# A gated decode block whose instructions a small recorder issues in place of the tile framework

## Chip, cores and metric

The kernel runs on one core of one Trainium2 chip. The metric is the time of one execution in device microseconds (us); before the change it is 376.34 us, the median of three runs (375.96 to 376.35). A profile of one further execution gives the instructions, the DMA transfers and the waits of that core. The engines are TensorE (PE; its weight loads are PEld), VectorE (DVE), ScalarE (ACT), GpSimd (POOL) and SyncE (SP). A q behind a name (SPq) means the engine's sequencer, which issues DMAs and handles semaphores.

## What is computed

One decode step for two sequences (B = 2, one token each, width D = 448): a layer norm, grouped-query attention over a cache of 4096 positions with 8 key heads and 16 query heads of width 256, and a bilinear gated feed-forward branch that multiplies the result of the attention.

```
xn = layernorm(x)                                     # 2 x 448
q  = xn @ wq                                          # 16 heads of 256, two per key head
p  = softmax(q . k_cache / 16)                        # over 4096 positions
s  = (p . v_cache) @ wo                               # 4096 -> 448
g  = silu(((xn @ w_gate) * (xn @ w_up)) @ w_down)     # 448 -> 1792 -> 448
out = x + s * g
```

All is float32. The two caches are 2 x 8 x 4096 x 256 numbers each, and every byte of them and of the weights is read once: the profile counts 158.56 MB read from memory.

## The kernel before

The work goes in 16 steps, one for each pair of a key head and a sequence (`N = 16`; `LAST = 14`). A step needs one key block and one value block, each 128 partitions by 8192 numbers (4 MB). `scores(i)` (L265) multiplies the query with the key block, 16 calls that appear as 32 matmul records, into a pair of PSUM banks, and DVE takes the maximum (L275). `softmax` (L285) spreads the maximum with two small matmuls (L287, L292), ACT takes the exponential (L295), and DVE transposes it (L298). `values(i)` (L309) multiplies that with the value block (L313). The loop (L366) runs `values(i)`, `scores(i + 1)`, the next loads, and `softmax(i + 1)`. The feed-forward branch and the second half of the queries run inside the loop at i = 0, 2 and 4, and the first half of the output projection at i = 8.

**Loads.** All loads but x are issued by SP in the order of the list `todo`. Two ring buffers hold 8 MB each: `v{i} k{i+1}` side by side, from the array vk. One slot holds the weights one after the other (wq0, then wgu, wdq, wo). The last two loads are cut: last0 (k15, v14) into two pieces, last1 (v15 and the rest of wo) into seven. `issue(n)` (L66) puts the next n of them on SP's queue; each waits there until the buffer that it overwrites has been read. There are 29 loads on SP (wq0, wqx, first, 14 of vk, wgu, wdq, wo, 2 of last0, 7 of last1), and two on ACT for the two rows of x (L106).

**Who orders the work.** Each engine runs its instructions in the order in which the program names them (`tc.manual_schedule()`). The tile framework allocates the buffers (L43 to L47), works out the dependencies, and sets the semaphores and waits. An instruction carries one wait; where it needs more, an EVENT_SEMAPHORE instruction in front of it carries them. The framework uses one counting semaphore for each compute engine and eight for DMAs in turn. A buffer that is allocated again waits for all readers of the whole old buffer.

**The two ends.** The program object (L471) starts with four constant fills on POOL and one meeting of all five engines: they drain and signal POOL, which releases them. Leaving the framework's context (L476) adds an end. SP waits for every semaphore of the framework, the store's among them; then the five engines meet, POOL clears the range of semaphores with one instruction, and the five meet again.

**The tail**, which the prediction follows: L313 for the last step, L410 (ACT scales the result), L322 (`combine`), L351 (`project`), L412 (DVE transpose), L356 (`project_last`), L239 (`spread`), L422 and L423 (gate and residual on DVE), and L424, the store of 57 KB on SP's queue.

```
    last ring load:   plan(f"v{LAST + 1} wo2", last1, [0, 4096, 7168, *(ROW + i * D for i in (0, 3, 6, 7, 8))])
    the end:          nc.vector.tensor_mul(gate, acc[:, :SL], gate)
                      nc.vector.tensor_add(gate, gate, xg)
                      nc.sync.dma_start(out, gate)
```

Of the kernel before, what the change touches and what calls it, by code (L numbers as in the profile page):

```python
# [1 line left out]

# [8 lines left out]
OP = mybir.AluOpType  # L11
# [24 lines left out]


# [3 lines left out]
@with_exitstack  # L41
def gated_decode_block(ctx: ExitStack, tc: tile.TileContext, x, first, vk, last0, last1, wq0, wqx, wdq, wo, wgu, out):
    nc = tc.nc  # L43
    ring = ctx.enter_context(tc.tile_pool(name="ring", bufs=2))
    slot = ctx.enter_context(tc.tile_pool(name="slot", bufs=1))
    const = ctx.enter_context(tc.tile_pool(name="const", bufs=1))
    work = ctx.enter_context(tc.tile_pool(name="work", bufs=2))  # L47
    psum = ctx.enter_context(tc.tile_pool(name="psum", bufs=1, space=bass.MemoryType.PSUM))
    ctx.enter_context(tc.manual_schedule())

    def two():
        return psum.tile([128, 2, 512], F32, name="s", bufs=2)


    def bank(name=None):
        return psum.tile([128, 512], F32, name=name, bufs=1) if name else two()[:, 0]


# [6 lines left out]
    def issue(n=1):  # L65
        for names, src, cuts in todo[:n]:  # L66
            weight = names[0].startswith("w")
            if weight:
                t = slot.tile([128, PART], F32, name="slot", align_bytes=512)
            else:  # L70
                t = ring.tile([128, 2 * ROW], F32, name="ring", align_bytes=512)
            width = ROW if not weight else src.shape[1] // len(names)
            for i, name in enumerate(names):
                loaded[name] = t[:, i * width:(i + 1) * width]
            if names == ["wd", "wq1"]:
                loaded["wd"], loaded["wq1"] = t[:, :14 * D], t[:, 14 * D:]
            for lo, hi in zip(cuts, cuts[1:]):
                nc.sync.dma_start(t[:, lo:hi], src[:, lo:hi])
            if names == ["wq0"]:
                at = src.shape[1]  # L80
                loaded["wqx"] = t[:, at:at + EXTRA * 512]
                nc.sync.dma_start(loaded["wqx"][:SIDE], wqx[:, :4])
        del todo[:n]
# [16 lines left out]
    def early():  # L100
        return [work.tile([128, 2, 512], F32, name=n, bufs=1)[:B] for n in ("p", "pT")]
# [3 lines left out]
    for b in range(B):  # L105
        nc.scalar.dma_start(x2[b:b + 1], x[b:b + 1])  # L106
    ident = const.tile([128, 128], F32)
    make_identity(nc, ident)
    one = const.tile([1, 1], F32)
    nc.vector.memset(one, 1.0)  # L110


    st = const.tile([B, 4], F32)
    xc = e0[:, 1, :D]
    sq = e1[:, 0, :D]
    eh = const.tile([B, 1], F32)
    nc.vector.memset(eh, -0.5)
    nc.vector.tensor_reduce(st[:, 0:1], x2, axis=AX.X, op=OP.add)
    nc.vector.tensor_scalar(st[:, 1:2], st[:, 0:1], 1.0 / D, None, op0=OP.mult)
    nc.vector.tensor_scalar(xc, x2, st[:, 1:2], None, op0=OP.subtract)  # L120
    nc.vector.scalar_tensor_tensor(sq, xc, 1.0, xc, op0=OP.mult, op1=OP.mult, accum_out=st[:, 2:3])  # L121
    nc.vector.tensor_scalar(st[:, 3:4], st[:, 2:3], 1.0 / D, EPS, op0=OP.mult, op1=OP.add)
    rstd = const.tile([B, 1], F32)
    nc.gpsimd.tensor_tensor(rstd, st[:, 3:4], eh, op=OP.pow)
# [3 lines left out]
    nc.vector.tensor_scalar(xn[:, :D], xc, rstd, None, op0=OP.mult)  # L128
    nc.vector.tensor_scalar(xn[:, D:D + LEFT], xc[:, D - LEFT:], rstd, None, op0=OP.mult)
    nc.vector.tensor_scalar(xn[:, D + LEFT:], xc[:, 384:D - LEFT], rstd, None, op0=OP.mult)  # L130
    pt = bank()
    for k in range(NK):
        nc.tensor.transpose(pt[:, B * k:B * (k + 1)], xn[:, k * 128:(k + 1) * 128], ident[:B, :B])  # L133
    def copies(dst, pt):
        n, b = pt.shape
        nc.vector.tensor_copy(dst.rearrange("p k (b j) -> p k b j", b=B),
                              pt.rearrange("p (k b) -> p k b", b=B)[:, :, :, None].to_broadcast([n, b // B, B, DUP]))

    xnT = const.tile([128, NK - 1, W], F32)
    copies(xnT, pt[:, :(NK - 1) * B])  # L140

    oT1 = const.tile([128, 3, 2, REP, W], F32)
# [3 lines left out]
    nc.vector.memset(xf, 0.0)  # L146
# [6 lines left out]
    for j in range(NS):  # L153
        at = 384 + j * SIDE
        nc.tensor.transpose(pt[:SIDE, B * j:B * (j + 1)], xn[:, at:at + SIDE], ident[:B, :B])
    nc.tensor.transpose(pt[:2 * LEFT, B * NS:B * (NS + 1)], xn[:, D - LEFT:D + LEFT], ident[:B, :B])
# [5 lines left out]
    nc.gpsimd.affine_select(out=xl, in_=xl, compare_op=OP.is_ge, fill=0.0, base=0, pattern=[[-LEFT, 2], [0, W]],  # L162
                            channel_multiplier=1)
    nc.gpsimd.affine_select(out=xl, in_=xl, compare_op=OP.is_ge, fill=0.0, base=LEFT - 1, pattern=[[LEFT, 2], [0, W]],
                            channel_multiplier=-1)

    both = work.tile([128, D], F32, name="h")[:B, :W].rearrange("p (b j) -> p b j", b=B)
    nc.vector.tensor_copy(both, ident[:B, :B, None].to_broadcast([B, B, DUP]))
    pt = bank()
    for c in range(NT):  # L170
        nc.tensor.matmul(pt[W * c:W * (c + 1), :SL], both.rearrange("p b j -> p (b j)"), x2[:, c * SL:(c + 1) * SL],
                         start=True, stop=True)
    xg = const.tile([128, SL], F32)
    nc.vector.tensor_copy(xg, pt[:, :SL])

    pick = const.tile([128, B], F32)
    nc.vector.tensor_reduce(pick, ident.rearrange("p (c b j) -> p b j c", c=NT, b=B)[:, :, 0, :], axis=AX.X, op=OP.add)
    rows4 = const.tile([128, 2, REP], F32)  # L180
    nc.vector.tensor_reduce(rows4.rearrange("p e r -> p (e r)"),
                            ident.rearrange("p (c f j) -> p f j c", c=NT, f=4)[:, :, 0, :], axis=AX.X, op=OP.add)
    add_head = const.tile([128, NT, REP, DUP], F32)
    nc.vector.tensor_copy(add_head, pick[:, None, :, None].to_broadcast([128, NT, REP, DUP]))

    add_step = const.tile([128, 2 * NT, REP, 8], F32)
    nc.vector.tensor_copy(add_step, pick[:, None, :, None].to_broadcast([128, 2 * NT, REP, 8]))
    add_blocks = const.tile([128, 2, REP, DUP], F32)
    nc.vector.tensor_copy(add_blocks, rows4[:, :, :, None].to_broadcast([128, 2, REP, DUP]))

    def rows(ps, w, n, extra=None):
# [5 lines left out]
        for k in range(3):  # L197
            for c in range(NT):
                nc.tensor.matmul(ps[W * c:W * (c + 1), :n], xnT[:, k, :], block(NT * k + c), start=k == 0, stop=False)  # L199
        def last(a, i):  # L200
            nc.tensor.matmul(ps[64 * a:64 * (a + 1), :n], xf.rearrange("p a j -> p (a j)"), block(i), start=False, stop=True)  # L201

        if extra is not None:

            for j in range(NS):
                for c in range(2):
                    at = (c * NS + j) * n
                    nc.tensor.matmul(ps[W * c:W * (c + 1), :n], xeT[:, j, :], extra[:SIDE, at:at + n], start=False, stop=False)  # L208
                if j == 0:
                    last(1, 12)  # L210
            nc.tensor.matmul(ps[:2 * W, :n], xl.rearrange("p a j -> p (a j)"), extra[:2 * LEFT, 2 * NS * n:(2 * NS + 1) * n],  # L211
# [6 lines left out]
    qT = [const.tile([128, B, 4, 2, REP, DUP], F32, name=f"qT{h}") for h in range(2)]  # L218

    def query(h):  # L220
        ps = bank()
        rows(ps, loaded[f"wq{h}"], 512, None if h else loaded["wqx"])
        for r in range(REP):
            nc.vector.transpose(qT[h][:, :, :, :, r, :].rearrange("p b g d j -> p (g d) b j"),
# [3 lines left out]
    gate = const.tile([128, SL], F32)  # L228
    hT = const.tile([128, 14, W], F32)


    def lift(ps):
        t = work.tile([128, D], F32, name="h")
        nc.vector.tensor_copy(t, ps[:, :D])
        return t

    def spread(t, dst, start, stop):
        for n in range(NT):
            nc.tensor.matmul(dst[W * n:W * (n + 1), :SL], add_head[:, 0].rearrange("p r j -> p (r j)"),  # L239
                             t[:, n * SL:(n + 1) * SL], start=start, stop=stop)  # L240

    def ffn_in():
# [3 lines left out]
        g = work.tile([128, FC], F32, name="h")  # L246
        nc.scalar.copy(g, pp[:, 0, :FC])
        h = work.tile([128, FC], F32, name="h")
        nc.vector.tensor_mul(h, pp[:, 1, :FC], g)
        nc.vector.transpose(hT.rearrange("p i m -> p (i m)"), h)  # L250

    def ffn_out():
        ps = bank()
        for i in range(14):
            t = i % NT
            nc.tensor.matmul(ps[W * t:W * (t + 1), :D], hT[:, i], loaded["wd"][:, i * D:(i + 1) * D],  # L256
# [3 lines left out]
        e = work.tile([128, D], F32, name="h")[:, :SL]  # L260
        nc.scalar.activation(e, y[:, :SL], AF.Sigmoid)
        nc.vector.tensor_mul(gate, y[:, :SL], e)


    def scores(i):  # L265
# [3 lines left out]
        m = work.tile([128, 2], F32, name="m", bufs=4)  # L269
        s = two()  # L270
        for h in range(2):
            for d in range(2):
                for c in range(NT):
                    nc.tensor.matmul(s[W * c:W * (c + 1), h, :], q[:, d], k[:, h, d, c, :], start=d == 0, stop=d == 1)  # L274
        nc.vector.tensor_reduce(m[:, 0:1], s, axis=AX.XY, op=OP.max)  # L275
# [3 lines left out]
    su = const.tile([128, N], F32)  # L279
# [5 lines left out]
    def softmax(i, s, m, pT=None):  # L285
        sm = bank("sm")
        nc.tensor.transpose(sm[:1, :128], m[:, 0:1], ident)  # L287
        mx = work.tile([1, NT, W], F32, name="mx", bufs=1)
        nc.vector.tensor_reduce(  # L289
            mx, sm[:1, None, :128].rearrange("p o (c j) -> p o j c", c=NT).to_broadcast([1, NT, W, NT]),  # L290
            axis=AX.X, op=OP.max)
        nc.tensor.transpose(sm[:, 128:129], mx.rearrange("p c j -> p (c j)"), one)  # L292
        nc.vector.tensor_scalar(m[:, 1:2], sm[:, 128:129], -1.0 / 16, None, op0=OP.mult)  # L293
        p = work.tile([128, 2, 512], F32, name="p", bufs=1)
        nc.scalar.activation(p, s, AF.Exp, bias=m[:, 1:2], scale=1.0 / 16, accum_out=su[:, place(i):place(i) + 1])  # L295
# [184 lines left out]
```

## Time and profile before

| what | us |
|---|---|
| time, median of 3 runs | 376.34 |
| the runs | 376.35, 376.34, 375.96 |
| span of the profiled execution, first to last instruction | 374.6 |
| PE busy (matmul) | 197.4 |
| DVE busy | 72.6 |
| ACT busy | 25.8 |
| POOL busy | 1.7 |
| mean granted TensorE clock | 0.775 |

The profiled execution has no other time on record than its span. The median of the runs is 1.7 us longer than that span; those 1.7 us lie ahead of the first instruction that the profile lists and behind the last one, and no row shows them. The page lists busy times by engine, the busy shares of 40 slices of the span, the DMA queues, the chain of work that ended last, and the costliest groups of instructions. Register, semaphore and DMA-issuing instructions do not count as busy; a query by line lists them.

### The profile page before, as it was taken

Reading aid. Unit: us, or ns where it says so; the run is one execution under the profiler, and the core shown is the slowest. Engines: PE = TensorE matmul, PEld = TensorE weight load, DVE = VectorE, ACT = ScalarE, POOL = GpSimd, SP = SyncE. Lnnn points to the kernel's source line nnn. Section 1 sums busy time; section 2 is a strip of 40 time slices with the busy share of each in tenths; the row PEclk is TensorE's granted clock in tenths of the full one; section 3 lists DMA queues with packets and bytes.
Section 4 is the critical chain, followed back from the end, with each engine's and each line's share of the span. In section 5 each row is a group of like instructions: output and inputs, shape, how many; then the busy total and the mean of one; then the engine's idle time right before and its main releaser. Section 6 shows DMA issues by size and latency. Waiting matters only on the chain.

```text
span 374.6 us, 3092 instructions
## 1 busy us (share of the span) xinstructions
PE 197.4 (53%) x1388; PEld 55.3 (15%) x1388; DVE 72.6 (19%) x125; ACT 25.8 (7%) x40; POOL 1.7 (0%) x9
## 2 busy tenths in 40 slices
PE   0793459081726090858271756712718180909785
PEld 0210112020201020212020211200202020202122
DVE  2303030104040003040404050400211212030530
ACT  1001010001020002010101010100010101010121
POOL 0000000000000000000000000000000000000000
PEclk9968596778696587796778696885868586777999
DMA  8999899999999999999999999999999999999994
GB/s 327 435 493 434 376 438 441 448 443 437 431 428 443 441 434 420 422 427 434 436 448 448 427 426 397 452 448 448 436 427 420 436 427 420 448 411 441 411 416 186
DMA packets 4217, 158.81 MB, mean 424 GB/s; under 512 B 599, under 2 KB 857, under 8 KB 1241
## 3 DMA queue, kind: packets, MB, share of 16 engines
q1 hardware_dynamic: 4201, 158.62, 98.2%
q8 instruction: 11, 0.18, 0.2%
q10 hardware_dynamic: 4, 0.00, 0.0%
q14 instruction: 1, 0.01, 0.0%
HBM read 158.56 MB, written 0.06 MB: 423 GB/s over the span
## 4 chain that ended last, share of the span: by engine, by line
DMA 74%; PE 23%; issue 1%; DVE 1%; ACT 0%; POOL 0%; ACTq 0%; SPq 0%; DVEq 0%
DMA ring<-vk 67%; PE o L313 10%; PE s L274 8%; DMA ring<-last 5%; DMA p<-x 2%; PE s L199 1%; PE s L208 1%; PE s L313 1%; PE s L211 1%; PE s L356 0%; PE s L201 0%; PE wide L351 0%; ACT ob L410 0%; PE cb L322 0%; DVE pT L121 0%
## 5 line engine op out<-in xcount | busy, mean ns | idle before, releaser
L313 PE MATMUL o<-ring,pT 128*32 128x512 f32 x480 | 83.2, 856 | 115.6 <-DMA ring<-vk 115.6
L275 DVE TENSOR_REDUCE m<-s 128x1 f32<-128x1024 f32 x16 | 19.6, 1222 | 219.9 <-PE s L274 219.9
L274 PE MATMUL s<-ring,qT 128*32 128x512 f32 x512 | 59.6, 607 | 0.9 <-PE s L211 0.9
L313 PEld LDWEIGHTS o<-ring,pT 128*32 128x32 f32 x480 | 20.8, 150 | 168.6 <-issue 156.1
L295 ACT ACTIVATE p<-s,m 128x1024 f32<-128x1024 f32 x16 | 17.8, 1113 | 286.1 <-DVE m L293 286.1
L274 PEld LDWEIGHTS s<-ring,qT 128*32 128x32 f32 x512 | 17.2, 112 | 40.7 <-issue 38.1
L298 DVE STREAM_TRANSPOSE pT<-p 128x1024 f32<-128x1024 f32 x15 | 18.7, 1245 | 21.2 <-ACT p L295 21.2
L199 PE MATMUL s<-slot,xnT 128*32 128x512 f32 (+1 forms) x96 | 15.3, 788 | 3.3 <-DMA slot<-wgu 3.3
L287 PE MATMUL sm<-ident,m 128*1 128x128 f32 x16 | 4.3, 270 | 18.8 <-DVE m L275 18.8
L289 DVE TENSOR_REDUCE mx<-sm 1x128 f32<-1x512 f32 x16 | 10.7, 671 | 2.9 <-PE sm L287 2.9
L292 PE MATMUL sm<-one,mx 1*128 1x1 f32 x16 | 3.6, 226 | 14.2 <-DVE mx L289 14.2
L373 DVE COPY ob<-o 128x512 f32<-128x512 f32 x14 | 9.5, 681 | 0.0
L256 PE MATMUL s<-slot,hT 128*32 128x448 f32 x28 | 5.8, 918 | 4.4 <-DMA slot<-wdq 4.4
L351 PE MATMUL wide<-slot,oT 128*32 128x448 f32 x48 | 6.4, 684 | 0.7 <-DVE oT L340 0.6
L287 PEld LDWEIGHTS sm<-ident,m 128*1 128x1 f32 x16 | 1.3, 79 | 32.9 <-DVE m L275 32.3
L133 PE MATMUL s<-ident,pT 2*128 2x2 f32 x4 | 0.6, 246 | 10.4 <-DVE pT L128 10.4
L322 PE MATMUL cb<-ob,add_blocks 128*32 128x512 f32 (+2 forms) x48 | 4.1, 456 | 2.4 <-DVE ob L373 1.6
L199 PEld LDWEIGHTS s<-slot,xnT 128*32 128x32 f32 x96 | 3.5, 137 | 11.7 <-issue 11.7
L292 PEld LDWEIGHTS sm<-one,mx 1*128 1x128 f32 x16 | 2.3, 142 | 17.2 <-DVE mx L289 17.2
L295 ACT ACT_TABLE_LOAD x2 | 2.6, 1283 | 30.6 <-DVE m L293 23.5
L313 PE MATMUL s<-ring,slot 128*32 128x512 f32 x32 | 4.2, 600 | 0.8 <-DMA ring<-last 0.8
L201 PE MATMUL s<-slot,oT 128*64 128x448 f32 (+1 forms) x14 | 4.6, 664 | 0.0
(76 smaller groups left out, 47.5 us busy)
## 6 DMA issues: line engine op xcount, KB each, us to landing
ring<-last SPq DMA_DIRECT2D x2, 4096.0 KB, 24.8
slot<-wdq SPq DMA_DIRECT2D x1, 6720.0 KB, 45.5
slot<-wgu SPq DMA_DIRECT2D x1, 6272.0 KB, 32.7
slot<-wo SPq DMA_DIRECT2D x1, 5376.0 KB
ring<-first SPq DMA_DIRECT2D x1, 4096.0 KB, 20.6
slot<-wq SPq DMA_DIRECT2D x1, 3328.0 KB, 10.7
ring<-last SPq DMA_DIRECT2D x1, 2048.0 KB
ring<-last SPq DMA_DIRECT2D x1, 1536.0 KB, 17.8
```

What stands on the lines that cost most here:

```text
L199: nc.tensor.matmul(ps[W * c:W * (c + 1), :n], xnT[:, k, :], block(NT * k + c), start=k == 0, stop=False)
L256: nc.tensor.matmul(ps[W * t:W * (t + 1), :D], hT[:, i], loaded["wd"][:, i * D:(i + 1) * D], start=i < NT, stop=i >= 14 - NT)
L274: nc.tensor.matmul(s[W * c:W * (c + 1), h, :], q[:, d], k[:, h, d, c, :], start=d == 0, stop=d == 1)
L275: nc.vector.tensor_reduce(m[:, 0:1], s, axis=AX.XY, op=OP.max)
L287: nc.tensor.transpose(sm[:1, :128], m[:, 0:1], ident)
L289: nc.vector.tensor_reduce(mx, sm[:1, None, :128].rearrange("p o (c j) -> p o j c", c=NT).to_broadcast([1, NT, W, NT]), axis=AX.X, op=OP.max)
L292: nc.tensor.transpose(sm[:, 128:129], mx.rearrange("p c j -> p (c j)"), one)
L295: nc.scalar.activation(p, s, AF.Exp, bias=m[:, 1:2], scale=1.0 / 16, accum_out=su[:, place(i):place(i) + 1])
L298: nc.vector.transpose(pT.rearrange("p h n -> p (h n)"), p.rearrange("p h n -> p (h n)"))
L313: nc.tensor.matmul(o[W * t:W * (t + 1), :], pT[:, h, at:at + 2 * W:2], loaded[f"v{i}"][:, e * 512:(e + 1) * 512], start=e < NT, stop=e >= ...
L351: nc.tensor.matmul(wide[W * t:W * (t + 1), :D], heads(oT, i, first), w, start=i < NT, stop=i >= SIDES - NT)
L373: nc.vector.tensor_copy(ob[:, place(i) % 8], o)
```

## The change

The tile framework goes. A class `Flow` records every call with the regions that it reads and writes, works out the waits, and issues everything at the end in the recorded order. Buffers become fixed allocations; a `Ring` hands them out in turn, and what must wait follows from overlapping regions and no longer from releases of whole buffers. The order of the calls on each engine stays, and so do shapes and operations. `make_identity` is written out as its two POOL instructions.

Semaphores: one for each compute engine that anyone waits for, and one for each DMA. Of the waits that an instruction needs, those that another of its waits implies are dropped; all but one go into instructions of their own ahead of it. Only instructions that someone waits for signal.

The end: SP waits for the last DVE instruction in an instruction of its own, issues the store with a semaphore `done`, clears the range of all other semaphores, waits for `done`, and clears that. There is no meeting of the engines behind the store, and SP alone has anything to do there.

```diff
-    with tile.TileContext(nc) as tc:
-        gated_decode_block(tc, *args, res)
+    gated_decode_block(nc, *args, res)
...
+    def record(self, engine, call, writes, reads, dma=False):
+        op = dict(engine=engine, call=call, needs=set(), wanted=False, dma=dma)
+        at = len(self.ops)
+        for ap, write in [(a, False) for a in reads] + [(a, True) for a in writes]:
...
+            psum = ap.space == bass.MemoryType.PSUM
+            for other, its, wrote in self.touched[ap.tensor.name]:
+                o = self.ops[other]
+                box = self.region(ap)
+                alone = psum and o["engine"] != engine
+                if alone:
+                    box, its = self.shared(box), self.shared(its)
...
+                if o["engine"] == engine and not o["dma"] and (engine == "PE" or not wrote):
+                    continue
+                op["needs"].add(other)
...
+    def settle(self):
...
+            need = [self.ops[o] for o in sorted(op["needs"], reverse=True)]
+            waits = {}
+            for o in need:
+                if known[e].get(o["lane"], 0) < o["n"]:
+                    if any(w["knew"].get(o["lane"], 0) >= o["n"] for w in waits.values()):
+                        continue
+                    if o["lane"] not in waits or waits[o["lane"]]["n"] < o["n"]:
+                        waits[o["lane"]] = o
...
+    def issue(self, final):
...
+        for op in self.ops:
+            e = op["engine"]
+            waits = [(sems[o["lane"]], o["mark"]) for o in op["waits"]]
+            while len(waits) > 1:
+                gate = self.engines[e].wait_ge(*waits.pop(0))
+                if len(waits) > 1:
+                    gate.wait_op(*waits.pop(0), "sem-ge")
+            if op is self.ops[-1]:
+                for w in waits:
+                    self.engines[e].wait_ge(*w)
+                op["call"]().then_inc(done, 16)
+                nums = sorted(s.num for s in sems.values())
+                assert nums == list(range(nums[0], nums[-1] + 1))
+                self.engines[e].sem_clear(range(nums[0], nums[-1] + 1))
+                self.engines[e].wait_ge(done, 16)
+                self.engines[e].sem_clear(done)
+                break
+            made = op["call"]()
+            for w in waits:
+                made.wait_op(*w, "sem-ge")
+            if op["wanted"]:
+                step = 16 if op["dma"] else 1
+                marks[op["lane"]] = op["mark"] = marks.get(op["lane"], 0) + step
+                made.then_inc(sems[op["lane"]], step)
...
-    make_identity(nc, ident)
+    POOL.memset(ident, 0.0)
+    POOL.affine_select(ident, in_=ident, compare_op=OP.not_equal, fill=1.0, base=0, pattern=[[-1, 128]],
+                       channel_multiplier=1)
...
-    nc.vector.tensor_mul(gate, acc[:, :SL], gate)
-    nc.vector.tensor_add(gate, gate, xg)
-    nc.sync.dma_start(out, gate)
+    DVE.tensor_mul(gate, acc[:, :SL], gate)
+    DVE.tensor_add(gate, gate, xg)
+    SP.dma_start(out, gate)
+    flow.issue(out)
```

All other lines of the diff replace `nc.vector`, `nc.tensor` and the like by the recorder's names, and framework allocations by fixed ones.

More of the change, by code (lines that the diff above doesn't have):

```diff
@@ new lines, with __init__, __getattr__, add @@
+class Recorder:
+    def __init__(self, flow, engine):
+        self.flow, self.engine = flow, engine
+    def __getattr__(self, name):
+        def add(out, *args, **kw):
+            reads = [a for a in [*args, *kw.values()] if isinstance(a, bass.AP)]
+            writes = [out]
+            if "accum_out" in kw:
+                writes.append(kw["accum_out"])
+                reads = [a for a in reads if a is not kw["accum_out"]]
+            method = getattr(self.flow.engines[self.engine], name)
+            self.flow.record(self.engine, lambda: method(out, *args, **kw), writes, reads, name == "dma_start")
+        return add
@@ new lines, in gated_decode_block, with sbuf, __init__, __call__ @@
+def gated_decode_block(nc, x, first, vk, last0, last1, wq0, wqx, wdq, wo, wgu, out):
+    flow = Flow(nc)
+    PE, DVE, ACT, POOL, SP = [getattr(flow, e) for e in ("PE", "DVE", "ACT", "POOL", "SP")]
+    names = iter(range(1000))
+    def sbuf(shape, name, align=32):
+        return nc.alloc_sbuf_tensor(f"{name}_{next(names)}", shape, F32, align_bytes=align)[:]
+    class Ring:
+        def __init__(self, name, shape, bufs, align=32):
+            self.bufs, self.n = [sbuf(shape, name, align) for _ in range(bufs)], 0
+        def __call__(self):
+            self.n += 1
+            return self.bufs[(self.n - 1) % len(self.bufs)]
+    ring = Ring("ring", [128, 2 * ROW], 2, 512)
+    slot = Ring("slot", [128, PART], 1, 512)
+    ident = sbuf([128, 128], "ident")
+    work = {n: Ring(n, s, b) for n, s, b in (
+        ("h", [128, D], 2), ("p", [128, 2, 512], 1), ("pT", [128, 2, 512], 1), ("m", [128, 2], 4),
+        ("mx", [1, NT, W], 1), ("ob", [128, 8, 512], 1))}
+    pairs = [nc.alloc_psum_tensor(f"s{i}", [128, 2, 512], F32)[:] for i in range(2)]
+    banks = {n: nc.alloc_psum_tensor(n, [128, 512], F32)[:] for n in ("wide", "sm", "o", "cb")}
@@ L51, in two @@
     def two():
-        return psum.tile([128, 2, 512], F32, name="s", bufs=2)
+        pairs.append(pairs.pop(0))
+        return pairs[-1]
     def bank(name=None):
-        return psum.tile([128, 512], F32, name=name, bufs=1) if name else two()[:, 0]
+        return banks[name] if name else two()[:, 0]
     N = HKV * B
@@ L100, in early @@
     def early():
-        return [work.tile([128, 2, 512], F32, name=n, bufs=1)[:B] for n in ("p", "pT")]
+        return [work[n]()[:B] for n in ("p", "pT")]
     e0, e1 = early()
@@ L114, in gated_decode_block @@
+    DVE.memset(one, 1.0)
+    st = sbuf([B, 4], "st")
     xc = e0[:, 1, :D]
     sq = e1[:, 0, :D]
[L116 to L122, printed above, removed]
@@ L161, in gated_decode_block @@
         copies(xl[:, a:a + 1], pt[:2 * LEFT, NS * B:(NS + 1) * B])
-    nc.gpsimd.affine_select(out=xl, in_=xl, compare_op=OP.is_ge, fill=0.0, base=0, pattern=[[-LEFT, 2], [0, W]],
+    POOL.affine_select(xl, in_=xl, compare_op=OP.is_ge, fill=0.0, base=0, pattern=[[-LEFT, 2], [0, W]],
                             channel_multiplier=1)
-    nc.gpsimd.affine_select(out=xl, in_=xl, compare_op=OP.is_ge, fill=0.0, base=LEFT - 1, pattern=[[LEFT, 2], [0, W]],
+    POOL.affine_select(xl, in_=xl, compare_op=OP.is_ge, fill=0.0, base=LEFT - 1, pattern=[[LEFT, 2], [0, W]],
@@ L183, in gated_decode_block @@
[L183 to L189, printed above, removed]
+    xg = sbuf([128, SL], "xg")
+    DVE.tensor_copy(xg, pt[:, :SL])
@@ L215, in rows @@
             last(a, 12 + a)
-    qT = [const.tile([128, B, 4, 2, REP, DUP], F32, name=f"qT{h}") for h in range(2)]
+    qT = [sbuf([128, B, 4, 2, REP, DUP], "qT") for h in range(2)]
     def query(h):
@@ L245, in ffn_in @@
             rows(pp[:, i], loaded[w], FC)
[L246 to L250, printed above, removed]
+        g = work["h"]()
+        ACT.copy(g, pp[:, 0, :FC])
+        h = work["h"]()
+        DVE.tensor_mul(h, pp[:, 1, :FC], g)
+        DVE.transpose(hT.rearrange("p i m -> p (i m)"), h)
     def ffn_out():
@@ L259, in ffn_out @@
         spread(lift(ps), y, True, True)
-        e = work.tile([128, D], F32, name="h")[:, :SL]
-        nc.scalar.activation(e, y[:, :SL], AF.Sigmoid)
-        nc.vector.tensor_mul(gate, y[:, :SL], e)
+        e = work["h"]()[:, :SL]
+        ACT.activation(e, y[:, :SL], AF.Sigmoid)
+        DVE.tensor_mul(gate, y[:, :SL], e)
     def scores(i):
@@ L268, in scores @@
         q = qT[g // 4][:, b, g % 4].rearrange("p d r j -> p d (r j)")
-        m = work.tile([128, 2], F32, name="m", bufs=4)
+        m = work["m"]()
         s = two()
@@ L273, in scores @@
                 for c in range(NT):
-                    nc.tensor.matmul(s[W * c:W * (c + 1), h, :], q[:, d], k[:, h, d, c, :], start=d == 0, stop=d == 1)
-        nc.vector.tensor_reduce(m[:, 0:1], s, axis=AX.XY, op=OP.max)
+                    PE.matmul(s[W * c:W * (c + 1), h, :], q[:, d], k[:, h, d, c, :], start=d == 0, stop=d == 1)
+        DVE.tensor_reduce(m[:, 0:1], s, axis=AX.XY, op=OP.max)
         return s, m
-    su = const.tile([128, N], F32)
+    su = sbuf([128, N], "su")
     def place(i):
@@ L350, in project @@
             w = loaded["wo"][:, i * D:(i + 1) * D] if i < LATE else loaded["wo2"][:, (i - LATE) * D:(i - LATE + 1) * D]
-            nc.tensor.matmul(wide[W * t:W * (t + 1), :D], heads(oT, i, first), w, start=i < NT, stop=i >= SIDES - NT)
+            PE.matmul(wide[W * t:W * (t + 1), :D], heads(oT, i, first), w, start=i < NT, stop=i >= SIDES - NT)
     def project_last(acc, o, i):
@@ L372, in gated_decode_block @@
         issue(1 + (i + 1 in weights))
-        nc.vector.tensor_copy(ob[:, place(i) % 8], o)
+        DVE.tensor_copy(ob[:, place(i) % 8], o)
         if i == LAST - 1:
@@ L398, in gated_decode_block @@
     project(oT1, 4, EARLY, LATE)
-    last = slot.tile([128, PART], F32, name="slot", align_bytes=512)
+    last = slot()
     p = softmax(LAST + 1, *ss, last[:, :1024].rearrange("p (h n) -> p h n", h=2))
```

211 lines of the change are left out of this document (130 added, 81 removed).

## The prediction

> **What bounds the kernel now.** I read the page first: the span, the DMA rows and the chain of work that ended last.
>
> ```profile
> span 374.6 us, 3092 instructions
> DMA  8999899999999999999999999999999999999994
> GB/s 327 435 493 434 376 438 441 448 443 437 431 428 443 441 434 420 422 427 434 436 448 448 427 426 397 452 448 448 436 427 420 436 427 420 448 411 441 411 416 186
> q1 hardware_dynamic: 4201, 158.62, 98.2%
> DMA 74%; PE 23%; issue 1%; DVE 1%; ACT 0%; POOL 0%; ACTq 0%; SPq 0%; DVEq 0%
> ```
>
> The transfers of SP's queue (q1) fill 98.2% of the time of the 16 DMA engines. The share is 8 or 9 tenths in every slice but the last. So the kernel is a stream of 158.62 MB with a short head and a tail. The chain still names PE for 23%, which asks for a second view: does the stream stop when PE works through a block? One block's work stands in the chain in order of time, and the windows show the DMA share (next to last column) at that place.
>
> ```profile
> 76.39 5.31 PE o L313 x32
> 81.71 3.48 PE s L274 x32
> 85.18 0.01 issue
> 85.20 46.14 DMA ring<-vk
> ```
>
> ```profile
> 75.00:80.00 5.00, 3.61 (x20) 1.06 (x24) 0.00 (x0) 0.00 (x0) 0.00 (x0) 0.52 0.97 419
> 80.00:85.00 5.00, 5.00 (x48) 1.35 (x40) 0.00 (x0) 0.00 (x0) 0.00 (x0) 1.00 0.99 423
> 85.00:90.00 5.00, 0.63 (x6) 0.21 (x2) 3.15 (x5) 1.20 (x2) 0.00 (x0) 1.00 1.00 433
> ```
>
> It does not stop. PE takes 5.31 + 3.48 = 8.8 us for a block, and meanwhile the next 8 MB, whose load was already in the queue, keep the share at 0.97 to 1.00. A block of 8.4 MB takes some 19.5 us at 430 GB/s, so a load that is issued up to 10 us later or earlier finds the queue full all the same. Only three places can move the time: the head, the tail behind the last data, and the stream's pace.
>
> The tail is read from the chain's last pieces.
>
> ```profile
> 347.69 17.79 DMA ring<-last
> 365.48 0.04 issue
> 365.52 2.30 PE s L313 x16
> 367.83 0.02 issue
> 367.85 0.70 ACT ob L410
> 368.55 0.04 issue
> 368.59 0.65 PE cb L322 x16
> 369.24 0.74 PE wide L351 x6
> 369.98 0.11 issue
> 370.09 0.78 PE s L356 x24
> 370.88 0.19 PE s L239 x8
> 371.07 0.47 PE s L356 x16
> 371.54 0.02 issue
> 371.56 0.28 DVE gate L422
> 371.85 0.02 issue
> 371.87 0.28 DVE gate L423
> ```
>
> From the landing at 365.5 to the end of L423 at 372.15 the engines pass work to each other with 0.02 to 0.11 us between them, 0.25 us in all. Behind it stand the store and the end, which the view of the waits, the timeline and the query of lines L424 and L476 show.
>
> ```profile
> 372.17 0.35 SPq L424 DMA_DIRECT2D res<-gate  x1
> ```
>
> ```profile
> DMA to landing us min/median/max: 1.6/1.6/1.6
> ```
>
> ```profile
> SPq L476 <- DMA res<-gate: 0.9, 1, 0.9
> SPq L476 <- ACTq L476: 0.4, 1, 0.4
> SPq L476 <- PEq L476: 0.2, 1, 0.2
> ```
>
> ```profile
> L476 SPq EVENT_SEMAPHORE  x8: 17/28/28, 372.6 to 374.5; - x8
> L476 POOLq EVENT_SEMAPHORE  x4: 17/17/17, 373.9 to 374.5; - x4
> ...
> L476 POOLq EVENT_SEMAPHORE_RANGE_CLEAR  x1: 96/96/96, 374.2 to 374.2; - x1
> ```
>
> The store is issued at 372.17 and lands 1.6 us later, at 373.77. Until then SP waits (0.9 us of it idle). From 373.77 to the end of the span at 374.6 there is no data left to move: those 0.8 us are the two meetings of the engines with POOL's clear of 0.096 us between them (SP waits 0.4 and 0.2 us in them).
>
> **The change part by part.** The profiled execution is the base: 374.6 us of span and, to the median of 376.34 us, 1.7 us around it.
>
> The head: nothing. The first load leaves behind the meeting of L471, which the diff does not touch, and the identity matrix stays two POOL instructions.
>
> ```profile
> SPq L471 <- PEq L471: 0.7, 1, 0.7
> ```
>
> ```profile
> 0.80 0.37 SPq L78 DMA_DIRECT2D slot<-wq  x1
> ```
>
> Loads in the middle: nothing. SP issues the same 29 loads in the same order. The 17 separate waits in front of loads (next fence) mostly go, since the reader's signal implies them; at 17 to 28 ns each, inside a wait for PE, that is worth nothing. Finer regions let k15 and three pieces of last1 start when `values` is done and not 3.48 us later after `scores`. The load ahead in the queue hides that. If this cover were gone, each of the 14 blocks would show up to 8.8 us of empty stream. A rule that held a load longer than now would have to hold it by over 10 us before it costs anything.
>
> ```profile
> L78 SPq EVENT_SEMAPHORE  x17: 17/17/28, 13.2 to 337.7; - x17
> ```
>
> Waits of PE, DVE and ACT: nothing. The order on each engine is the same and every data dependency stays. PE no longer waits for itself. The new rule that two engines in one PSUM bank wait for each other, readers too, matters only where both work on one bank at a time; in the tail each bank passes from PE to its reader anyway. In the tail there are ten handovers; a gate more or less at 0.03 us each, and at most ten of them, bounds the sum to between -0.25 (all the gaps shown) and +0.3 us. I take 0, since the same pairs of engines meet in the same order.
>
> The store: its wait becomes an instruction of its own. SP gets through five EVENT_SEMAPHOREs between 372.6 and 372.8, that is about 0.05 us each. It now starts 0.02 us behind L423; I add 0.05 us (0 to 0.1).
>
> ```profile
> L476 SPq EVENT_SEMAPHORE  x5: 17/28/28, 372.6 to 372.8; - x5
> ```
>
> The clear under the store: 35 semaphores (31 DMAs and four engines). POOL's one instruction for a range took 0.096 us. From the end of the issue, 372.5, to the landing, 373.8, SP has 1.2 us. One instruction of 0.1 us is hidden; the third rival takes it otherwise.
>
> The end: the 0.8 us behind the landing go (374.6 less 373.77 is 0.83). In their place come the end of the wait (0.03 us, the row of 28 ns) and the clear of `done` (0.10, as POOL's). That is 0.13 us, between 0.05 (two EVENT_SEMAPHOREs) and 0.3 (a clear with the drains around it, 374.1 to 374.4). The span so loses 0.83 - 0.13 - 0.05 = 0.65 us and becomes 373.9 to 374.0.
>
> Around the span: unknown. PE, ACT, POOL and DVE are through with the program before the store lands, and no longer wait for a release. What each must do afterwards, within the 1.7 us, they can do while SP still waits. It cannot get longer by that: SP's own part is as long as before, and the others come earlier. So the loss is 0; the gain lies between 0 and 0.6 us, the sum of the two waits in the meetings above. I take 0.2, the shorter of the two, since a single early handover is nearer to one meeting than to both.
>
> The Trainium skill's page Runtime: NRT & Kernel Launch, section The ~15µs preamble/postamble breakdown, says that the runtime wraps the program in a barrier of its own, a chain through the five engines of about 0.355 us (44 ns a hop), and resets 51 semaphores per engine. No row here shows either. By it the removed meetings and clear are done a second time after the span, and as an estimate from its hops up to four of eight would be passed early, 0.18 us; the sum with that in place of 0.2 would be the same within 0.02.
>
> Sum: 0.65 + 0.2 = 0.85 us less. From the median, 376.34 - 0.85 = **375.5 us**. By the ends of each term: best -0.83 + 0.05 + 0 - 0.6 - 0.25 = -1.6 (374.7), worst -0.83 + 0.3 + 0.1 + 0 + 0.3 = -0.1 (376.2).
>
> **The rivals.** *The time around the span stays whole.* The steps behind the last instruction begin when SP is done and take their 1.7 us whoever else is early. For it: no row shows them shorter. Against it: four of five engines have 0.8 us or more of lead over SP, where now all leave within the last 0.2 us. Only the 0.65 us count: 375.7. The same page of the Trainium skill, in that section, gives the closing barrier as a stage of its own of about 1.5 us that waits for all engines; taken as a fixed price, it stands for this rival.
>
> *One meeting stays.* L471 shows that a meeting comes from the program object and not from the framework; a layer below could close every program in that way, and the rows of L476 cannot tell whose each meeting is. Then the change does only half of what it says, 0.4 us more are paid: 376.34 - 0.65 + 0.4 = 376.1. Against it: the rows of L476 are whole without it, two meetings with one clear between.
>
> *The clear goes one by one, and the kernel is slower.* If clearing a range on SP costs as much as an EVENT_SEMAPHORE for each of 35 semaphores, 0.05 to 0.06 us each, it takes about 2 us, from 372.6 to 374.6, with 0.1 for `done` behind it; the end is then at 374.8, 0.2 later than now: 376.5. At POOL's 0.096 us each it is 3.4 us, and the time 377.9. It hides up to 1.2 / 35 = 0.034 us each, and turns the result beyond (1.2 + 0.65) / 35 = 0.053 us. For it: the range is three times longer than the framework's and a different engine clears it. Against it: POOL did a whole range in 0.096 us.
>
> *The stream's pace.* All buffers move to other addresses, and the slowest stretch shows what a dip costs.
>
> ```profile
> 40.00:45.00 5.00, 2.73 (x16) 0.87 (x20) 0.00 (x0) 0.00 (x0) 0.00 (x0) 0.50 0.81 351
> ```
>
> At 351 instead of 424 GB/s (158.62 MB over 374.6 us) these 5 us lose 0.86 us. One such dip more or less gives 376.4 or 374.6, two more 377.2. For it: the tail's last pieces hang on the data, so it counts in full. Against it: the bytes, their order and their queue stay.
>
> **How the numbers follow.** The forecast has 0.42; the time around the span whole (375.7) 0.20; one meeting left (376.1) 0.13; the clear one by one 0.08; the pace 0.17, half of it each way. A difference of 0.2%, 0.75 us here, is about what a measurement of this kernel can tell from no change, so faster means below 375.6 and slower above 377.1. Faster: 0.38 of the forecast, 0.05 of the second case, whose 375.7 lies near the bound, and 0.08 of the pace, 0.51. Slower: 0.04 of the clear, 0.09 of the pace and 0.01 of the third case, 0.14. The rest, 0.35, is the same. The range 375.0 to 376.4 holds the forecast between its likelier ends and the second and third case; it leaves out the clear and most of the pace, about 0.2.
>
> **What would show it.** Right: a span near 374.0; no EVENT_SEMAPHORE or DRAIN on PE, DVE, ACT or POOL behind the store; on SP a wait for the store of about 1.1 us and one clear before and one after it; DMA shares by window as now; a time 1.5 us above the span. Wrong: rows of clears past 373.8, a DRAIN on five engines at the end, a gap in the stream near a load's issue, or a last landing of the loads away from 365.5.

## The result, and the profile after

The time fell from 376.13 us (median of 9 runs, 375.95 to 376.66) to 374.95 us (9 runs, 374.71 to 375.62), a ratio of 0.997 with a 95% interval of 0.9961 to 0.998. The forecast was 375.5 us, 0.85 us less than the median of 376.34 that it started from; measured were 1.2 us less than the 376.13. One later run of the kernel before, at 411.66 us, is left out of all ratios, spans and times less span below. The profiled execution after the change took 374.99 us, with a span of 373.7.

The page of the kernel after has the same stream as before.

```profile
span 373.7 us, 3019 instructions
DMA  8999899999999999999999999999999999999995
GB/s 322 449 480 435 375 441 449 449 437 433 392 475 435 442 407 428 437 435 442 442 437 428 428 430 422 455 437 435 428 428 428 430 442 449 437 389 431 428 413 221
q1 hardware_dynamic: 4201, 158.62, 98.4%
DMA 75%; PE 22%; DVE 1%; issue 0%; ACT 0%; POOL 0%; ACTq 0%; DVEq 0%
```

The packets and bytes of q1 are the same to the last digit, and its share is 98.4% where it was 98.2%. (All recorded calls now bear the recorder's line, L164, so groups go by tiles.) The stretch with one block's work, by windows, DMA share next to last:

```profile
75.00:80.00 5.00, 3.68 (x20) 0.99 (x24) 0.00 (x0) 0.00 (x0) 0.00 (x0) 0.50 0.97 419
80.00:85.00 5.00, 5.00 (x44) 1.25 (x40) 0.00 (x0) 0.00 (x0) 0.00 (x0) 0.83 0.99 423
85.00:90.00 5.00, 1.55 (x14) 0.37 (x6) 2.56 (x4) 0.95 (x1) 0.00 (x0) 0.85 1.00 433
```

The shares 0.97, 0.99 and 1.00 are those of before. The tail, from the chain of the kernel after:

```profile
365.46 2.30 PE s L164 x16
367.76 0.02 issue
367.79 0.70 ACT ob L164
368.49 0.04 issue
368.53 0.64 PE cb L164 x16
369.17 0.75 PE wide L164 x6
369.92 0.03 issue
369.95 1.53 PE s L164 x48
371.48 0.03 issue
371.50 0.28 DVE gate L164
371.78 0.02 issue
371.81 0.28 DVE gate L164
```

It starts 0.06 us earlier and runs piece for piece as before. What differs lies behind it. The timeline, the query of the store's line, SP's waits, and the queries of the two clears:

```profile
372.11 0.35 SPq L164 DMA_DIRECT2D res<-gate  x1
```

```profile
DMA to landing us min/median/max: 1.6/1.6/1.6
```

```profile
SPq L139 <- DMA res<-gate: 1.1, 1, 1.1
```

```profile
L137 SPq EVENT_SEMAPHORE_RANGE_CLEAR  x1: 91/91/91, 372.5 to 372.5; - x1
```

```profile
L139 SPq EVENT_SEMAPHORE_RANGE_CLEAR  x1: 25/25/25, 373.7 to 373.7; - x1
```

The store leaves 0.02 us behind the last DVE instruction, lands 1.6 us later at 373.7, and one instruction of 25 ns ends the program. No other engine has a row behind the store: the last rows of the four, by engine, are these.

```profile
12.35 0.54 POOL L164 TENSOR_SCALAR_AFFINE_SELECT oT<-oT 8x64 f32<-8x64 f32 x2 [2.44 <-DVE oT L164]
369.98 0.53 ACT L164 COPY h<-wide 128x448 f32<-128x448 f32 x1 [1.50 <-PE wide L164]
370.78 0.66 PE L164 MATMUL s<-ring,oT 128*32 128x112 f32 x16
371.81 0.28 DVE L164 TENSOR_TENSOR gate<-gate,xg 128x112 f32<-128x112 f32 x1
```

The clear of the 35 semaphores takes 91 ns in the store's shadow. The span shrank by 374.6 - 373.7 = 0.9 us. The rest is around the span: the profiled execution's time is 374.99 - 373.7 = 1.29 us above its span. Before, that difference could only be formed with the median of other runs (1.7); the experiments give it run by run.

### The profile page after: what moved, and what is told of

It is laid out like the page before. It is cut to its first block, busy times and chain, and to the rows that moved or that the text cites. A ratio compares the mean times of both kernels' runs of the same rounds, so it can differ in the third digit from the quotient of the medians.

```text
span 373.7 us, 3019 instructions
## 1 busy us (share of the span) xinstructions
PE 192.1 (51%) x1388; PEld 50.8 (14%) x1388; DVE 72.9 (19%) x125; ACT 25.9 (7%) x40; POOL 1.7 (0%) x9
## 3 DMA queue, kind: packets, MB, share of 16 engines
q1 hardware_dynamic: 4201, 158.62, 98.4%
## 4 chain that ended last, share of the span: by engine, by line
DMA 75%; PE 22%; DVE 1%; issue 0%; ACT 0%; POOL 0%; ACTq 0%; DVEq 0%
DMA ring<-vk 68%; PE s L164 11%; PE o L164 10%; DMA ring<-last 6%; DMA p<-x 2%; DVE pT L164 0%; DVE qT L164 0%; DVE st L164 0%; DVE oT L164 0%; PE wide L164 0%; ACT ob L164 0%; PE cb L164 0%; DVE gate L164 0%; POOL rstd L164 0%; ACTq L164 0%
## 5 line engine op out<-in xcount | busy, mean ns | idle before, releaser
L164 PE MATMUL o<-ring,pT 128*32 128x512 f32 x480 | 82.5, 850 | 121.4 <-DMA ring<-vk 121.4
L164 DVE TENSOR_REDUCE m<-s 128x1 f32<-128x1024 f32 x16 | 19.6, 1222 | 226.9 <-PE s L164 226.9
L164 PE MATMUL s<-ring,qT 128*32 128x512 f32 x512 | 59.5, 607 | 1.1 <-DVE qT L164 1.1
L164 PEld LDWEIGHTS o<-ring,pT 128*32 128x32 f32 x480 | 18.5, 149 | 175.8 <-DMA ring<-vk 125.8
L164 ACT ACTIVATE p<-s,m 128x1024 f32<-128x1024 f32 x16 | 17.8, 1116 | 321.0 <-DVE m L164 321.0
L164 DVE STREAM_TRANSPOSE pT<-p 128x1024 f32<-128x1024 f32 x15 | 18.7, 1245 | 19.1 <-ACT p L164 19.1
L164 PEld LDWEIGHTS s<-ring,qT 128*32 128x32 f32 x512 | 16.1, 112 | 41.5 <-issue 39.5
L164 PE MATMUL s<-slot,xnT 128*32 128x512 f32 (+1 forms) x96 | 14.4, 751 | 2.3 <-DMA slot<-wgu 2.3
L164 PE MATMUL sm<-ident,m 128*1 128x128 f32 x16 | 4.3, 270 | 19.0 <-DVE m L164 19.0
L164 DVE TENSOR_REDUCE mx<-sm 1x128 f32<-1x512 f32 x16 | 10.7, 670 | 2.9 <-PE sm L164 2.9
L164 PE MATMUL sm<-one,mx 1*128 1x1 f32 x16 | 3.7, 231 | 14.2 <-DVE mx L164 14.2
L164 DVE COPY ob<-o 128x512 f32<-128x512 f32 x14 | 9.5, 681 | 0.0
L164 PE MATMUL s<-slot,oT 20*32 20x512 f32 (+3 forms) x28 | 7.9, 593 | 0.0
L164 PE MATMUL s<-slot,hT 128*32 128x448 f32 x28 | 5.0, 827 | 3.1 <-DMA slot<-wdq 3.1
L164 PE MATMUL s<-ident,pT 2*128 2x2 f32 (+2 forms) x8 | 0.7, 203 | 10.4 <-DVE pT L164 10.4
L164 PEld LDWEIGHTS sm<-ident,m 128*1 128x1 f32 x16 | 1.3, 79 | 33.0 <-DVE m L164 32.4
L164 PE MATMUL wide<-slot,oT 128*32 128x448 f32 x48 | 4.9, 543 | 1.4 <-DMA slot<-wo 0.9
L164 PE MATMUL cb<-ob,add_blocks 128*32 128x512 f32 (+2 forms) x48 | 4.1, 456 | 2.4 <-DVE ob L164 1.6
L164 PE MATMUL s<-ring,slot 128*32 128x512 f32 x32 | 4.2, 600 | 1.7 <-DMA ring<-last 1.7
L164 PEld LDWEIGHTS s<-slot,xnT 128*32 128x32 f32 x96 | 3.3, 137 | 10.4 <-issue 8.0
L164 PEld LDWEIGHTS sm<-one,mx 1*128 1x128 f32 x16 | 2.4, 147 | 17.2 <-DVE mx L164 17.2
```

The lines of the kernel that those rows point to most:

```text
L164: self.flow.record(self.engine, lambda: method(out, *args, **kw), writes, reads, name == "dma_start")
```

## The experiments

**Theory.** The whole gain lies at the end: 0.8 to 0.9 us of the span are the two meetings and the clear, and 0.45 us around the span are gained because four engines are through early. **Rivals.** The recorder's waits or its finer release of buffers give part of the gain; or the time around the span is shorter for another reason, such as fewer instructions.

All kernels below are the kernel after with another end, but for the first. "Time less span" is taken for each run; the table gives the median and the extremes, and the lowest span, since the spans of each kernel scatter upwards (last section).

| run | ratio to before, 95% interval | median us | lowest span | time less span |
|---|---|---|---|---|
| before, its 33 runs beside the first four | | 376.29 | 374.3 | 1.74 (1.68 to 1.85) |
| after, first result | 0.997 (0.9961 to 0.998) | 374.95 | 373.5 | 1.29 (1.21 to 1.35) |
| a_before_again | 0.9998 (0.9989 to 1.0007) | 376.27 | 374.4 | 1.74 (1.68 to 1.81) |
| b_full_end | 1.0008 (0.9998 to 1.0018) | 376.80 | 374.4 | 1.71 (1.70 to 1.88) |
| c_one_meeting | 0.9996 (0.9987 to 1.0005) | 376.47 | 373.8 | 1.76 (1.70 to 1.81) |
| d_all_wait | 0.9984 (0.9975 to 0.9993) | 375.77 | 373.6 | 1.77 (1.72 to 1.86) |
| e_pool_waits | 0.9981 (0.9972 to 0.9989) | 375.58 | 373.5 | 1.87 (1.75 to 1.93) |
| f_pe_waits | 0.9979 (0.9969 to 0.999) | 375.27 | 373.6 | 1.55 (1.46 to 1.63) |
| g_clear_each | 1.0 (0.9992 to 1.0009) | 376.26 | 374.4 | 1.29 (1.23 to 1.39) |
| h_clear_each_late | 1.0019 (1.0011 to 1.0028) | 377.05 | 375.5 | 1.26 (1.21 to 1.35) |
| i_after_again | 0.9956 (0.9943 to 0.9969) | 374.94 | 373.5 | 1.26 (1.24 to 1.36) |
| j_full_end_again | 1.0 (0.9991 to 1.0008) | 376.29 | 374.3 | 1.77 (1.69 to 1.87) |

**The kernel before, again.**

> The kernel before, unchanged, to have the span of each of its runs beside its time. Theory (the whole gain lies at the end): time 376.1 us, spans near 374.5, and the time stands 1.7 to 1.9 us above the span in every run. Rival (the steps around the span are the same for both kernels and the stream got faster): time less span is 1.3 us, as in the kernel after, and the spans are near 374.8.

Measured: spans from 374.4, and 1.74 us above the span. The rival fell: the time around the span does differ between the two kernels, 1.74 against 1.29 us.

**The old end on the new kernel.**

```diff
-                self.engines[e].sem_clear(range(nums[0], nums[-1] + 1))
                 self.engines[e].wait_ge(done, 16)
-                self.engines[e].sem_clear(done)
+                nc.all_engine_barrier()
+                nc.gpsimd.sem_clear(range(nums[0], nums[-1] + 1))
+                nc.gpsimd.sem_clear(done)
+                nc.all_engine_barrier()
```

> The kernel after, with the old end put back behind the store: SP waits for the store, the five engines meet, POOL clears, the five meet again. All else is the recorder's. Theory (only the end counts): ratio to before 0.999 to 1.001, time 375.9 to 376.3, span 374.4 to 374.6, time less span 1.7 to 1.9. Rival (the recorder's waits and its finer release of buffers give part of the gain): 375.5 or less with the old end in place.

> The recorder with the old end, a second time, since 7 of 11 runs of the first had spans of 375.0 and more, where its lowest was 374.4. Theory (the recorder's other parts give and cost nothing; such runs come in every kernel here): lowest span 374.4, time less span 1.7 to 1.85, ratio 0.999 to 1.001. Rival (the recorder costs something, which its end more than pays back): ratio 1.001 to 1.002 with an interval clear of 1.

Measured: 1.0008 and then 1.0000 (0.9991 to 1.0008), with a lowest span of 374.4 and 374.3, where the kernel before has 374.3. With the old end the gain is gone. So the recorder, its waits and its finer buffers give nothing that these runs can tell: the interval of j is 0.1% either way, that of b reaches 0.2% slower. The many high spans of b did not come again. The end put back is not quite the old one: POOL's clear of 35 semaphores takes 225 ns in b, where the framework's range took 96. From the start of the store to the end of the span the profile of j has 2.44 us and that of before 2.39, so this hides some 0.05 us. The clear of b, and SP's waits in j, with the same two meetings behind the store:

```profile
L139 POOLq EVENT_SEMAPHORE_RANGE_CLEAR  x1: 225/225/225, 374.7 to 374.7; - x1
```

```profile
SPq L137 <- DMA res<-gate: 1.2, 1, 1.2
...
SPq L141 <- PEq L141: 0.5, 1, 0.5
SPq L138 <- PEq L138: 0.2, 1, 0.2
```

**The kernel after, again.**

> The kernel after, unchanged, on one chip with the old end put back (next run). Theory (all of the gain lies at the end, 0.85 us in the span and 0.45 around it): lowest span 373.5, time less span 1.2 to 1.35, ratio to before 0.996 to 0.998.

Measured on the same chip as j: 0.9956 (0.9943 to 0.9969). The ratio lies just below the 0.996 to 0.998 expected, as the median of before was high there, at 376.44; the lowest span is 373.5 and the time less span 1.26, as expected. Between i and j lie 0.8 us of lowest span and 0.5 us around it.

**One meeting.**

```diff
                 self.engines[e].sem_clear(done)
+                nc.all_engine_barrier()
```

> The kernel after, with one meeting of the five engines behind SP's last clear. Theory (the steps around the span get shorter because four engines are through early; a meeting takes that lead away): span 373.7 + 0.4 = 374.1, time less span back at 1.7 to 1.8, time 375.8 to 375.9. Rival (the steps around the span are shorter for another reason, as fewer instructions or semaphores): span 374.1, time less span 1.3, time 375.4.

Measured: 1.76 us around the span, so the theory's part of it holds. One meeting costs 0.3 us of lowest span (373.8 against 373.5, where 0.4 was expected) and takes back 0.47 us around it. The expected time of 375.8 to 375.9 lies among the runs (lowest 375.53), the median of 376.47 above it: 6 of its 11 runs have high spans (0.45 us or more above the lowest).

**No meeting, but no engine through early.**

```diff
-                self.engines[e].wait_ge(done, 16)
-                self.engines[e].sem_clear(done)
+                for other in ("SP", "PE", "DVE", "ACT", "POOL"):
+                    self.engines[other].wait_ge(done, 16)
```

> The kernel after, in which PE, DVE, ACT and POOL also wait for the store's semaphore, each in one instruction, with no meeting and without the clear of that semaphore. The span hardly grows, but no engine is through early. Theory (the lead of the four shortens the steps around the span): span 373.7, time less span 1.7 to 1.8, time 375.4 to 375.5. Rival (the lead counts for nothing): span 373.7, time less span 1.3, time 375.0.

The query of the wait's line shows all five engines leaving together:

```profile
L139 SPq EVENT_SEMAPHORE  x1: 17/17/17, 374.7 to 374.7; - x1
L139 ACTq EVENT_SEMAPHORE  x1: 17/17/17, 374.7 to 374.7; - x1
L139 POOLq EVENT_SEMAPHORE  x1: 17/17/17, 374.7 to 374.7; - x1
L139 DVEq EVENT_SEMAPHORE  x1: 21/21/21, 374.7 to 374.7; - x1
L139 PEldq EVENT_SEMAPHORE  x1: 51/51/51, 374.7 to 374.7; - x1
```

Measured: lowest span 373.6, and 1.77 us around the span. One wait on each of four engines adds almost nothing to the span and brings back 0.48 us that no row shows. That tells the theory from its second rival: the instructions are those of the kernel after, but for four waits more and a clear less, and still the time around the span is that of before. The runs g and h below point the same way: there SP alone runs 34 instructions more, and the time less span stays at 1.29 and 1.26 us. The lead of the other engines over SP is what counts, and 2 us more of it, in h, give nothing further.

**Which engine's lead.** In the next two only one of the four waits (`for other in ("SP", "POOL")`, then `("SP", "PE")`; the rest as in d).

> The kernel after, in which POOL alone, besides SP, also waits for the store's semaphore (the semaphore is not cleared). With all four waiting, time less span was 1.77 us; with none 1.29. Theory that the slowest engine to leave decides, and that it is POOL: time less span 1.7 to 1.8. Theory that each of the four has a share: 1.4. Theory that any one late engine costs the whole: 1.7 to 1.8 here and with PE alone. The span stays at 373.6 in undisturbed runs in each.

> The kernel after, in which PE alone, besides SP, also waits for the store's semaphore. If the slowest engine to leave decides and that is POOL: time less span between 1.3 and 1.55. If PE is the slowest: 1.7 to 1.8, and less for POOL alone. If each of the four has a share: 1.4. If any one late engine costs the whole: 1.7 to 1.8 in both.

Measured: 1.87 us with POOL alone, 1.55 with PE alone, against 1.29 with none and 1.77 with all. POOL alone brings back all of it, PE a good half, so the engines do not add up. That fits the theory that the latest of them decides and that of these two it is POOL.

That POOL alone costs 0.1 us more than all four together was not expected. The traces explain some 0.04 us of it, if each profile stands for its kernel's runs. The span of d ends with PE's wait, 0.04 us behind POOL's; in before, b, c and j PE's last row ends 0.09 us behind POOL's. Counted from the end of POOL's last row, the medians become 1.81 us in d, 1.83 in before, 1.80, 1.85 and 1.86 in b, c and j, and 1.87 in e: nearly the same wherever POOL is held to the end, with a clear of `done` or without. In f only PE is held, and no run leaves out the clear of `done` and nothing else; so a part of its 0.26 us could come from that. ACT and DVE alone were not tried.

**The price of the clears.** Under the store first:

```diff
-                self.engines[e].sem_clear(range(nums[0], nums[-1] + 1))
+                for n in nums:
+                    self.engines[e].sem_clear(range(n, n + 1))
```

> The kernel after, with the range of 35 semaphores cleared by 35 instructions under the store. Third rival of the prediction, priced at 0.05 to 0.06 us each: about 2 us from 372.5, that is 0.8 us past the landing of the store, span 374.5 to 374.6, time 375.7 to 375.9. If each takes only the 0.025 us of the clear of one semaphore: hidden under the store, span 373.6, time 375.0.

Then the same 35 clears behind the wait for the store:

> The kernel after, with the same 35 single clears behind the wait for the store, so that nothing hides them. At 0.05 to 0.06 us each the span grows by 1.8 to 2.1 us, to 375.5 and time 376.8; at 0.025 us each by 0.9 us. Against the run with the clears under the store the difference is what the store hides, 1.2 us.

The rows of the clears, in g and in h:

```profile
L138 SPq EVENT_SEMAPHORE_RANGE_CLEAR  x35: 25/30/39, 372.4 to 374.4; - x35
```

```profile
L139 SPq EVENT_SEMAPHORE_RANGE_CLEAR  x35: 25/30/34, 374.0 to 376.0; - x35
```

From the first start to the last, 34 steps take 1.97 us in both traces, 0.058 us each, though the row counts 0.030 us for one. Under the store they stick out by 0.9 us of lowest span (374.4 against 373.5), and the median is level with before: 1.0 (0.9992 to 1.0009). By lowest span and time less span a gain of some 0.35 us would be left (374.4 + 1.29 = 375.7 against 374.3 + 1.73 = 376.0 for the runs of before beside it); 7 of the 12 runs of g have high spans, which hides it in the median. Behind the store the kernel is slower than before, by 0.19% (0.11 to 0.28). Between the two lie 1.1 us of lowest span: that is what the store hides. For the one clear of the range the store hides its 91 ns, and the choice of one instruction for the range is worth 0.9 us.

## Why the prediction was right, and where it was not

**The bound was right.** Stream, tail and order are unchanged, and the whole change is in what follows the store's landing. The prediction costed the loads, the waits and the head at nothing. The run j with the old end confirms the sum of these, within 0.1%. It missed that the engines' own work, PE's above all, makes a path nearly as long as the data's (last section). The finer release does issue the last nine loads earlier, as the prediction said; the rows of before and of after:

```profile
L78 SPq DMA_DIRECT2D ring<-last x9: 328/426/434, 327.1 to 350.1; - x9
```

```profile
L164 SPq DMA_DIRECT2D ring<-last x9: 327/328/450, 322.9 to 345.6; - x9
```

They were queued 4.2 to 4.5 us earlier, and the tail began at 365.46 in place of 365.52: the load ahead in the queue hid it.

**The old end** was put at 0.83 us of span. The lowest spans of j and i differ by 0.8, and those of before and after by 0.8 to 0.9.

**The new end was costed too high, by 0.10 us.** The prediction took 0.03 us for the wait and 0.10 for the clear of `done`. There is one instruction, which carries the wait and takes 25 ns; POOL's 0.096 us had been for a whole range.

**The store's own wait was costed at 0.05 us and costs nothing.** The step read the wait in the program's text as an instruction of SP's. In the trace there is none: the wait goes with the DMA, which starts at 372.11, 0.02 us behind DVE's end at 372.09, as before.

**Around the span is the term that was mis-sized.** The prediction took 0.2 of a bound of 0 to 0.6 us, the shorter of the two waits in the meetings. It measured 0.45 (1.74 less 1.29). The mechanism was the right one, as c and d show. What failed is the choice within the bound, which no row supported: the step compared what SP waits for in a meeting, while what counts, as e and f suggest, is how long the latest engine needs from its last instruction until it is done, and that has no row. With POOL it is longer than with PE, and in the kernel after POOL's last row ends at 12.9 us. The sum becomes 0.83 - 0.03 + 0.45 = 1.25 us in place of 0.85, or 375.1; from the median of nine runs, 376.13, it gives 374.9.

The Trainium skill's page Runtime: NRT & Kernel Launch, section The ~15µs preamble/postamble breakdown, gives the closing barrier as a stage of about 1.5 us that waits for all engines. No row here separates that stage, so its price stays open; as a fixed price for the whole time around the span it does not agree with these runs, where the median of the time less span moves between 1.26 and 1.87 us with the engine that ends last. The prediction's estimate of 0.18 us from the hops was too small too, against 0.45.

**The rivals.** The time around the span did not stay whole (1.29, not 1.7). No meeting stayed; c shows that one would have cost 0.3 us in the span and the 0.47 around it, so the rival's 376.1 would have been about 375.7. The clear did not go one by one, but its price of 0.05 to 0.06 us each was right: it is 0.058. The time and the turning point worked out from it were not, since both left out the term around the span: the turning point of 0.053 becomes (1.2 + 0.83 - 0.03 + 0.45) / 35 = 0.07 with the measured terms, and in place of the rival's 376.5 the runs of g have a median of 376.26 and a lowest of 375.73. (At 0.096 us each the prediction's own terms give 377.8, not 377.9.) The pace did not change.

## What to carry to other kernels

When the last store is all that is left, every instruction that the waiting engine runs behind its landing is paid in full (35 clears, 2.0 us of span): let one engine wait for it, and put the clearing under it, in one instruction for the range. Let the other engines run out of program early: here that gave 0.45 us on top of the 0.8 us of the meetings. A single instruction on POOL that waits for the last store took it back here (run e). Compare a run's time with its own span before and after such a change, because a part of the gain has no row.

## What the runs showed of the hardware that was not expected

The spans of every kernel scatter upwards. Counting runs that lie 0.45 us or more above the lowest span of their kernel in the same measurement, they are 33 of 91 for the kernel before and 40 of 100 for all with the recorder, so nothing here says that the change has a part in it. The profiled run of d is one of them, with a span of 374.8 and a lowest of 373.6. Its windows stand first, those of the kernel after second (granted TensorE clock third from the end):

```profile
350.00:355.00 5.00, 4.23 (x30) 1.04 (x26) 1.39 (x3) 1.21 (x2) 0.00 (x0) 0.54 0.99 426
355.00:360.00 5.00, 5.00 (x40) 1.13 (x32) 3.16 (x6) 0.00 (x0) 0.00 (x0) 0.78 0.99 420
```

```profile
350.00:355.00 5.00, 3.83 (x34) 1.07 (x33) 3.26 (x8) 1.21 (x2) 0.00 (x0) 1.00 0.96 416
355.00:360.00 5.00, 4.11 (x38) 1.32 (x42) 2.52 (x5) 1.21 (x2) 0.00 (x0) 1.00 0.97 413
```

The clock was 0.54 and 0.78 in these 10 us, where it was 1.00; the data came as fast. The chain of d does not name the last loads: from 337.64 us to the end it names the work of PE, DVE and ACT, and the score block in it took longer:

```profile
352.98 5.68 PE s L164 x32
```

The same 32 matmuls in the kernel after, from its timeline:

```profile
350.96 3.64 PE L164 MATMUL s<-ring,qT 128*32 128x512 f32 x32
```

The profile of c, with a span of 375.5, is like that: the same block takes 5.74 us, at 0.60 and 0.72. So this tail, bound by data in nine of the twelve profiles, was bound by the engines' work, PE's above all, in these two, whose clock was low from 350 to 360 us. The third, j, has a chain of the engines' work too, with 0.76 and 1.00 in those 10 us, and a low span of 374.4: the two paths are nearly equally long. The high profile of b is of another kind: its tail began with the last data at 366.23 in place of 365.46. What sets either in a given run is open. The Trainium skill's page TensorE: Matmul & The Clock Gate, section Part 1: The HAM clock gate, says that the gate judges activity in a free-running window and so differs from run to run. The rows agree that far: 0.54 and 1.00 at the same place of the same work.
